# Amid-attention MLP blocks of 384 tokens with the output chunks in two passes over groups of four activation tiles

## The chip, the cores and the metric

The kernel runs on one core of a Trainium2 chip. The metric is the device time in microseconds, the median of three runs. In the core, TensorE (PE) multiplies, VectorE (DVE), ScalarE (ACT) and GpSimd (POOL) work element by element, SyncE (SP) issues most of the DMAs. Each engine runs its instructions in the order in which the program holds them and waits at semaphores for what others produce.

## The reference

Attention with a memory term over 4 batches of 576 tokens and 8 heads of width 64, then two MLPs over the 2304 tokens of 512 values:

```
scores = scale * q @ k.T, causal;  local = softmax(scores) @ v
q_p = phi(q);  mem_out = (q_p @ M_prev) / (q_p . z_prev + 1e-6)
x = g * mem_out + (1 - g) * local                 # (2304, 512)

h = x @ w_in                                      # 512 -> 2048
x = (s * relu(h) ** 2 + b) @ w_out                # 2048 -> 512
h = x @ w2_in
x = (P(h) / (Q(h) + 1e-6)) @ w2_out               # P cubic, Q of |h| and h * h
```

The MLP weights arrive as 64-bit floats and are decoded on the chip. Every MLP operand is split into a high and a low half (type fp32r), and a product is three matmuls: low by high, high by low, high by high.

## The kernel before

Nothing is ordered by hand. The code describes operations (`op`, with the engines that may do them and the planner's cost on each, the tiles read and written, and a due time `plan.at`), and `Plan.run` plays a list schedule: at each step the operation that can start first is placed, ties by due time, and on the engine where it ends first by the planner's costs. So the order on each engine, and for many operations the engine itself, comes out of the planner. The order is fixed when the program is built.

Attention has 32 units (4 batches, a low round of query tiles 0 to 2 and a high round of 3 and 4, 4 head pairs). A unit's names: `s` and `su` scores in PSUM, `p` and `pu` the exponentials, `rs` their sums, `pt` and `th` transposed exponentials in PSUM and SBUF, `qm`, `ph`, `tz`, `c`, `pf`, `fs`, `fl` the phi branch (`fs` and `fl` its high and low half), `mh` and `ml` the halves of the memory matrix, `av` the output in PSUM, `xp` its copy, stored to `xTd`.

While attention runs, the first MLP's first half of hidden features (`wA`: 8 tiles `f` of 128) is worked for the first `NARROW * BA` = 768 tokens, by `block_a`, in blocks of `BA` tokens. A block loads its input (`take`: raw `xr`, halves `xh`, `xl`); `up(f)` makes 12 matmuls into a bank `ha` of PSUM (4 chunks of the input by 3); `relu_square` makes from it `r` on ACT, the square on DVE, the high half `gha` on ACT or DVE, the low half `gla` on DVE; `down` makes 3 matmuls for each of the 4 output chunks into `acc`, summed over the 8 tiles `f`. At the end `acc` is copied to `ev` and stored to `x2p`.

Before, a block has 256 tokens, and two tiles `f` share a bank `ha` side by side, so the element-wise work is 512 wide. The four output chunks share two banks, (0) and (1), two chunks in each, and hold them from the block's first down matmul to its last:

```
                ACC = f"acc{j}_{q}"
                if i == 0:
                    bank(ACC, (q,))
```

All banks but 0 and 1 are free for attention and `ha` (`FREE`). Then `block_wide` does the same for the other 1536 tokens (512 at a time: `hw`, `aw`), `block_b` the second half of the features (`hb`, `ab`), and `block_c` the second MLP (`hc`, `ac`).

Due times: attention's units are `TIMES[0]` apart (1.2 times that in the high rounds); the blocks are due evenly between `FIRST_A` = 90 and the planner's end of attention:

```
    tA = [FIRST_A + k * (END - LAST_A - FIRST_A) / NARROW for k in range(NARROW + 1)]
```

Tiles in SBUF come from rings of named places (`roles`): `gh` 3, `gl` 2, `ev` 2 in the pool `mp`; the pool `at` holds attention's tiles and is closed after it (`swap`).

## Time and profile before

| | us |
|---|---|
| median of 3 runs (1021.85 to 1024.05) | 1023.35 |
| the profiled execution: time | 1023.09 |
| its span, first to last instruction | 1021.3 |
| PE busy in the span | 994.9 |
| DVE, ACT, POOL busy | 840.2, 675.9, 426.3 |
| attention and the amid-attention blocks | about 0 to 290 |
| the other 1536 tokens of the first half | about 290 to 415 |
| the second half of the features | about 415 to 622 |
| the second MLP | about 622 to 1021 |

The page gives busy time by engine. The views of the trace used here: busy time of each engine by stretches (with the number of instructions, the granted TensorE clock as a share of full speed, the share of the DMA engines and their rate), the waits of PE (who waited for whom, total us, times, longest), the chain of work that ended last in order of time, and groups of instructions by line, operation and shape. In these a group's row ends with its busy time, the mean of one in ns, and the idle time of the engine just before. The chain's pieces give the sustained time of a matmul: a run of matmuls by their number. The mean of one matmul is longer, since its pipeline overlaps the next one's.

### The profile page before, as it was taken

What the parts mean: (1) busy time and instruction counts of PE and PEld (TensorE: products, weight loads), DVE (VectorE), ACT (ScalarE), POOL (GpSimd) and SP (SyncE); (2) the same over time, 40 slices, a digit from 0 to 9 for tenths busy, and PEclk for the clock granted to TensorE, in tenths of its full rate; (3) what the DMA queues carried; (4) which work ended last, traced back from release to release, by engine and by line L of the source; (5) the groups of instructions that cost most, each with busy time, mean ns of one, the idle gap of its engine ahead of it and who ended that gap; (6) DMA issues with size and microseconds to landing.
All of it is one profiled execution on the core that took longest, in us unless ns stands there. A gap on an engine that the chain in (4) does not pass through costs nothing.

```text
span 1021.3 us, 16000 instructions
## 1 busy us (share of the span) xinstructions
PE 994.9 (97%) x5356; PEld 828.1 (81%) x5356; DVE 840.2 (82%) x1524; ACT 675.9 (66%) x1419; POOL 426.3 (42%) x494
## 2 busy tenths in 40 slices
PE   7889899999999999999999999999999999999998
PEld 4566687877888888887888998888888888899997
DVE  7999899898858888889887336988888888888895
ACT  6889888677654554444444326777777867877885
POOL 3235344131100100212110006868777876876785
PEclk8999999999999999999999999999999999999999
DMA  7866766554213647767564028401100200100000
GB/s 203 248 210 193 211 202 184 145 157 125 82 49 113 187 145 247 249 201 248 162 210 132 26 84 257 144 1 32 50 1 3 70 1 1 65 2 0 32 1 31
DMA packets 68962, 120.07 MB, mean 118 GB/s; under 512 B 9744, under 2 KB 36880, under 8 KB 68880
## 3 DMA queue, kind: packets, MB, share of 16 engines
q1 hardware_dynamic: 64224, 110.27, 35.2%
q0 software_dynamic: 4224, 8.39, 2.6%
q8 instruction: 42, 0.69, 0.3%
q10 hardware_dynamic: 432, 0.40, 0.1%
q14 instruction: 40, 0.33, 0.1%
HBM read 91.76 MB, written 27.26 MB: 117 GB/s over the span
## 4 chain that ended last, share of the span: by engine, by line
PE 83%; DVE 9%; DMA 3%; ACT 2%; issue 1%; POOL 1%; SPq 0%; DVEq 0%; ACTq 0%; POOLq 0%
PE hc L876 19%; PE ac L1111 19%; PE ab L1025 9%; PE hb L876 8%; PE hw L876 6%; PE aw L988 6%; PE ha L876 3%; PE av L820 3%; PE pt L512 3%; PE acc L949 2%; PE s L640 2%; DVE s L647 1%; PE av L828 1%; DMA qm<-in_vm 1%; PE su L674 1%
## 5 line engine op out<-in xcount | busy, mean ns | idle before, releaser
L1090 DVE RECIPROCAL qe<-qe 128x512 f32<-128x512 f32 (+2 forms) x82 | 242.6, 2958 | 49.2 <-POOL qe L382 49.2
L876 PE MATMUL hc<-xc_h,w2ih 128*128 128x512 f32 (+1 forms) x320 | 117.8, 368 | 0.0
L876 PE MATMUL hc<-xc_h,w2il 128*128 128x512 f32 (+1 forms) x320 | 117.8, 368 | 0.0
L876 PE MATMUL hc<-xc_l,w2ih 128*128 128x512 f32 (+1 forms) x320 | 117.7, 368 | 0.0
L382 POOL TENSOR_TENSOR qe<-qe,qb 128x512 f32<-128x512 f32 (+2 forms) x82 | 94.9, 1157 | 52.4 <-ACT qb L1075 51.3
L1111 PE MATMUL ac<-w2oh,ghc 128*128 128x512 f32 x288 | 112.6, 391 | 0.0
L1111 PE MATMUL ac<-w2ol,ghc 128*128 128x512 f32 x288 | 112.5, 391 | 0.0
L1111 PE MATMUL ac<-w2oh,glc 128*128 128x512 f32 x288 | 112.3, 390 | 0.0
L382 POOL TENSOR_TENSOR glc<-po,ghc 128x512 fp32r<-128x512 f32 (+2 forms) x82 | 95.0, 1158 | 23.3 <-ACT ghc L372 23.1
L382 POOL TENSOR_TENSOR pm<-pm,s 128x512 f32<-128x512 f32 (+2 forms) x82 | 95.5, 1165 | 18.7 <-ACT pm L1075 17.8
L1081 ACT ACTIVATE s<-hc 128x512 f32<-128x512 f32 (+2 forms) x82 | 44.7, 546 | 63.3 <-PE hc L876 60.6
L658 ACT ACTIVATE p<-s,st 128x128 f32<-128x128 f32 (+3 forms) x128 | 67.0, 537 | 19.4 <-DVE st L647 17.5
L1075 ACT ACTIVATE pm<-hc,prm 128x512 f32<-128x512 f32 (+2 forms) x82 | 59.6, 727 | 24.4 <-DVE hc L1092 24.0
L512 PE MATMUL pt<-ident,p 128*128 128x128 f32 x320 | 59.4, 286 | 9.7 <-DVE fl L742 4.7
L876 PEld LDWEIGHTS hc<-xc_h,w2il 128*128 128x128 f32 x320 | 60.1, 188 | 9.0 <-DVE po L1094 0.3
L876 PEld LDWEIGHTS hc<-xc_l,w2ih 128*128 128x128 f32 x320 | 60.1, 188 | 8.5
L876 PEld LDWEIGHTS hc<-xc_h,w2ih 128*128 128x128 f32 x320 | 60.0, 188 | 7.5
L647 DVE CUSTOM_DVE_ANT_0 s<-s,mask 128x128 f32<-128x128 f32 (+3 forms) x128 | 60.4, 507 | 4.6 <-ACT p L658 2.4
L1075 ACT ACTIVATE qb<-s,cq,b1abs 128x512 f32<-128x512 f32 (+2 forms) x82 | 62.7, 764 | 2.1 <-POOL qe L382 2.1
L1111 PEld LDWEIGHTS ac<-w2oh,ghc 128*128 128x128 f32 x288 | 54.1, 188 | 11.4
L1111 PEld LDWEIGHTS ac<-w2oh,glc 128*128 128x128 f32 x288 | 54.1, 188 | 11.1 <-POOL glc L382 0.6
L1111 PEld LDWEIGHTS ac<-w2ol,ghc 128*128 128x128 f32 x288 | 54.1, 188 | 10.4
(488 smaller groups left out, 2795.8 us busy)
## 6 DMA issues: line engine op xcount, KB each, us to landing
qk<-in_qk SPq DMA_DIRECT2D x32, 208.0 KB, 3.9
vm<-in_vm SPq DMA_DIRECT2D x16, 384.0 KB, 4.2
qk<-in_qk SPq DMA_DIRECT2D x30, 192.0 KB, 3.9
out_y<-ob SPq DMA_DIRECT2D x18, 256.0 KB, 2.1
qm<-in_vm SPq DMA_DIRECT2D x16, 256.0 KB, 3.7
w2d<-sh SPq DMA_DIRECT2D x16, 256.0 KB, 4.3
w2d<-sl SPq DMA_DIRECT2D x16, 256.0 KB, 4.0
w2oh<-w2d POOLq DMA_DIRECT2D x4, 1024.0 KB, 16.4
```

The source lines that it names most:

```text
L382: op(ways(c, None, dve, pool), lambda e: e.tensor_tensor(dst(), x(), y(), alu), r, w, port=True)
L512: nc.tensor.transpose(dst[:, o:o + P], src, ident)
L647: e.tensor_tensor_reduce(sp, sp, mask[:, m0:m0 + kb - ka], -scale, 3.0e38 if x == 0 else st[:, t:t + 1], ALU.add, ALU.min, st[:, t + x:t + ...
L658: e.activation(g(f"p{n}_{i}")[:, o:o + kb - ka], g(b)[:, o2:o2 + kb - ka], AF.Exp, scale=-1.0, bias=g(f"st{n}")[:, z_:z_ + 1], accum_out=g ...
L820: nc.tensor.matmul(g(AV)[64 * j:64 * j + 64, ra:rb], g(V)[:, kb, D * j:D * j + D], g(TH)[:, o:o + rb - ra], start=x in firsts, stop=False, ...
L876: nc.tensor.matmul(hs(), m, y, start=c == 0 and k == 0, stop=c == KC - 1 and k == 2)
L988: nc.tensor.matmul(g(ACC)[:, 0:w], outp(y, f)[:, cs], g(z_), start=f == 0 and k == 0, stop=f == HF - 1 and k == 2)
L1025: nc.tensor.matmul(g(ACC)[:, 0:w], outp(y, f)[:, cs], g(z_), start=f == 0 and k == 0, stop=f == HF - 1 and k == 2)
L1075: return lambda e: e.activation(g(dst)[:, ks], g(src)[:, ks], AF.Identity, scale=m, bias=b)
L1081: op(ways(c, -0.04), lambda e, ks=ks: e.activation(g(S2)[:, ks], g(HS)[:, ks], AF.Square), (HS,), part(S2))
L1090: op({"DVE": 0.07 + c * 0.00625}, lambda e, ks=ks: e.reciprocal(g(QE)[:, ks], g(QE)[:, ks]), part(QE), part(QE))
L1111: nc.tensor.matmul(g(ACC), g(x_)[:, ks], g(f"w2o{y}{i}")[:, o], start=f == 0 and q == 0, stop=f == NF - 1 and q == 2)
```

## The change

- A block has 384 tokens, and there are two (`BA`, `NARROW`): the same 768 tokens. A matmul of these blocks has 384 columns for 256.
- Each tile `f` has a bank `ha` of its own, 384 wide; `relu_square` works 384 wide, 16 times for 12.
- An output chunk is 384 wide and fills its own bank. The two banks serve chunks 0 and 1, then 2 and 3, over the tiles `f` 0 to 3 (`GROUP` = 4); then again over 4 to 7. So the halves of four activation tiles stay in SBUF for both passes: `gha` and `gla` have rings of 5, partly in the attention pool.
- After the first group a chunk is copied from PSUM to `ev` (4 tiles of 384); after the second it is added to `ev` by a DVE `tensor_tensor` that reads PSUM and SBUF, and stored.
- `up` and `down` no longer alternate: chunk pairs and ups stand in a list `todo`, due times spread by weight 2 for an up and 1 for a pair of downs.
- Attention's due times are 8.3 apart for 8.5.

```diff
@@ -43,7 +43,7 @@
 LANDS, LANDS_RAW, LANDS_CB = 1.0, 2.5, 2.5
 ALONE = 8
 R0, R1, RN = 0.0, 0.0, 0
-NARROW = 3
+NARROW, GROUP = 2, 4
 LATE = 512, 512, 512
 FIRST_A, LAST_A = 90.0, 0.0
 SOON = 1
@@ -53,7 +53,7 @@
 D0, D1, D2, D3 = 40.0, 5.0, 80.0, 5.0
 TINYPOOL = 0.12
 DIRECT, GATE, MPLAIN = 4, 1.0, 4
-TIMES = 8.5, 8.0, 1.2
+TIMES = 8.3, 8.0, 1.2
 VAL, PHB, BGAP = 1.0, 1.0, 0.15
 DEC = 20.0
 SB0, SB1, SB2, SB3, N2 = 85.0, 25.0, 110.0, 16.0, 8
@@ -270,7 +270,7 @@
     nks = [min(q + P, S) for q in q0s]
     NQ = len(q0s)
     SQ = NQ * P
-    BA = 256
+    BA = 384
 
     pools = {}
 
@@ -313,6 +313,7 @@
         buf(n, None, obj=t)
     both = at.tile([P, 64], F32, name="both")
     nc.vector.tensor_tensor(both, ident[:, 0:64], ident[:, 64:128], ALU.add)
+    at.tile([P, 32], F32, name="fill_at")
     prm = cst.tile([P, 8], F32, name="prm")
     sb = cst.tile([P, 2], F32, name="sb")
     sc1, bi1 = sb[:, 0:1], sb[:, 1:2]
@@ -878,12 +879,12 @@
             first = [] if not c and not part else [(HS, part if c else 0)]
             pe(3 * w, mm, first + [XH, XL, kh, kl], ((HS, part),), 3)
 
-    def relu_square(HS, hs, w, nm):
+    def relu_square(HS, hs, w, nm, gh="gh", gl="gl"):
 
         R, GH, GL = f"r{nm}", f"gh{nm}", f"gl{nm}"
         ring(R, "r", [P, w], F32)
-        ring(GH, "gh", [P, w], F32R)
-        ring(GL, "gl", [P, w], F32R)
+        ring(GH, gh, [P, w], F32R)
+        ring(GL, gl, [P, w], F32R)
 
         def relu(e):
             e.activation(g(R), hs(), AF.Relu)
@@ -915,51 +916,60 @@
 
     def block_a(j, at0, at1, inp, outp):
 
-        t0 = j * BA
+        t0, w = j * BA, BA
         plan.at = at0 - LOADS
-        x = take(f"xa{j}", BA, tok_runs(t0, BA))
+        x = take(f"xa{j}", w, tok_runs(t0, w))
         parts = {}
 
-        def up(i):
-            HS = f"ha{j}_{i}"
+        def up(f):
+            HS = f"ha{j}_{f}"
             bank(HS, FREE)
-            for u in range(2):
-                f = 2 * i + u
-                fs = slice(f * P, (f + 1) * P)
-                up_matmuls(HS, lambda u=u: g(HS)[:, u * BA:(u + 1) * BA], BA, x,
-                           lambda c, f=f: (("w1ihA", (c, f // 4)), ("w1ilA", (c, f // 4))),
-                           lambda y, c, fs=fs: inp(y, c, fs), u)
-            parts[i] = relu_square(HS, lambda: g(HS), 512, f"a{j}_{i}")
-
-        def down(i):
-            GH, GL = parts[i]
-            for q in range(2):
-                ACC = f"acc{j}_{q}"
-                if i == 0:
-                    bank(ACC, (q,))
-                for c in (2 * q, 2 * q + 1):
-                    cs = slice(c * P, (c + 1) * P)
-                    for u in range(2):
-                        f = 2 * i + u
-
-                        def mm(ACC=ACC, c=c, cs=cs, u=u, f=f):
-                            a = g(ACC)[:, (c % 2) * BA:(c % 2 + 1) * BA]
-                            us = slice(u * BA, (u + 1) * BA)
-                            for k, (y, z_) in enumerate((("l", GH), ("h", GL), ("h", GH))):
-                                nc.tensor.matmul(a, outp(y, f)[:, cs], g(z_)[:, us],
-                                                 start=f == 0 and k == 0 and c % 2 == 0,
-                                                 stop=f == HF - 1 and k == 2, skip_group_check=True)
-
-                        first = f == 0 and c % 2 == 0
-                        pe(3 * BA, mm, ([] if first else [ACC]) + [GH, GL, ("w1ohA", f), ("w1olA", f)], (ACC,), 3)
-                if i == HF // 2 - 1:
-                    EV = f"ev{j}_{q}"
-                    ring(EV, "ev", [P, 512], F32)
-                    copy(lambda EV=EV: g(EV), lambda ACC=ACC: g(ACC), 512, (ACC,), (EV,), act=-0.04)
-                    load(lambda q=q: x2p[q * 2 * P:(q + 1) * 2 * P, t0:t0 + BA].rearrange("(c p) t -> p c t", p=P),
-                         lambda EV=EV: g(EV).rearrange("p (c t) -> p c t", c=2), 512 * 512, (EV,), (("x2p", j),))
-
-        interleave(HF // 2, 1, up, down, at0, at1)
+            fs = slice(f * P, (f + 1) * P)
+            up_matmuls(HS, lambda: g(HS)[:, 0:w], w, x, lambda c: (("w1ihA", (c, f // 4)), ("w1ilA", (c, f // 4))),
+                       lambda y, c: inp(y, c, fs))
+            parts[f] = relu_square(HS, lambda: g(HS)[:, 0:w], w, f"a{j}_{f}", "gha", "gla")
+
+        def down(f, cs):
+            GH, GL = parts[f]
+            h, k4 = divmod(f, GROUP)
+            for c in cs:
+                ACC, EV = f"acc{j}_{h}_{c}", f"ev{j}_{c}"
+                ms = slice(c * P, (c + 1) * P)
+                if k4 == 0:
+                    bank(ACC, (c % 2,))
+
+                def mm(ACC=ACC, ms=ms):
+                    for k, (y, z_) in enumerate((("l", GH), ("h", GL), ("h", GH))):
+                        nc.tensor.matmul(g(ACC)[:, 0:w], outp(y, f)[:, ms], g(z_), start=k4 == 0 and k == 0,
+                                         stop=k4 == GROUP - 1 and k == 2)
+
+                pe(3 * w, mm, ([ACC] if k4 else []) + [GH, GL, ("w1ohA", f), ("w1olA", f)], (ACC,), 3)
+                if k4 < GROUP - 1:
+                    continue
+                if h == 0:
+                    ring(EV, "eva", [P, w], F32)
+                    copy(lambda EV=EV: g(EV), lambda ACC=ACC: g(ACC)[:, 0:w], w, (ACC,), (EV,), act=-0.04)
+                else:
+                    op(ways(w, None, 1.0), lambda e, ACC=ACC, EV=EV: e.tensor_tensor(
+                        g(EV), g(ACC)[:, 0:w], g(EV), ALU.add), (ACC, EV), (EV,))
+                if h == HF // GROUP - 1:
+                    load(lambda c=c: x2p[c * P:(c + 1) * P, t0:t0 + w], lambda EV=EV: g(EV), 512 * w, (EV,), (("x2p", j),))
+
+        todo = [(up, (0,))]
+        for h in range(HF // GROUP):
+            f0 = h * GROUP
+            for f in range(f0, f0 + GROUP):
+                if h == 0 and f + 1 < GROUP:
+                    todo.append((up, (f + 1,)))
+                todo.append((down, (f, (0, 1))))
+            for f in range(f0, f0 + GROUP):
+                if f + GROUP < HF:
+                    todo.append((up, (f + GROUP,)))
+                todo.append((down, (f, (2, 3))))
+        cost = [2.0 if fn is up else 1.0 for fn, _ in todo]
+        for i, (fn, args) in enumerate(todo):
+            plan.at = at0 + (at1 - at0) * sum(cost[:i]) / sum(cost)
+            fn(*args)
 
     def block_wide(t0, w, at0, at1, inp, outp):
 
@@ -1128,6 +1138,9 @@
         "gh": [("mp", f"gh{i}") for i in range(3)], "gl": [("mp", f"gl{i}") for i in range(2)],
         "r": [("mp", "r")], "ev": [("mp", f"ev{i}") for i in range(2)],
     })
+    roles["gha"] = [("mp", "gh0"), ("mp", "gh1"), ("mp", "gh2")] + [("at", f"gx{i}") for i in range(GROUP - 2)]
+    roles["gla"] = [("mp", "gl0"), ("mp", "gl1")] + [("at", f"gy{i}") for i in range(GROUP - 1)]
+    roles["eva"] = [("mp", "ev0"), ("mp", "ev1"), ("at", "ex0"), ("at", "ex1")]
     NPR = len(units)
 
     TL, TS, TR = TIMES
```

In the built program PE has 192 matmuls fewer: 576 of 256 columns in the blocks become 384 of 384. Of this stage's element-wise instructions, DVE has 863 before and 848 now, ACT 565 and 578, POOL 177 and 209; the loads of block input are 8 and 12, the stores 6 and 8.

Two places in the order. First PE at the end of the last block. Before, its last down matmuls (`acc`, chunks 2 and 3 in bank 1) stand among the last unit's steps:

```order
L949 MATMUL acc_1_3852<-gha_3_4292,w1olA 128x256
L949 MATMUL acc_1_3852<-gla_3_4303,w1ohA 128x256
L949 MATMUL acc_1_3852<-gha_3_4292,w1ohA 128x256
L949 MATMUL acc_1_3852<-gha_3_4292,w1olA 128x256
L949 MATMUL acc_1_3852<-gla_3_4303,w1ohA 128x256
L949 MATMUL acc_1_3852<-gha_3_4292,w1ohA 128x256
L512 MATMUL pt_0_4448<-ident,p_0_4367 128x128
L791 MATMUL pt_0_4448<-ident,pu_4401 128x2x64
L512 MATMUL pt_0_4448<-ident,p_0_4380 128x128
L512 MATMUL pt_0_4448<-ident,pu_4401 128x128
```

Now, at the same end, `acc_1_0` and `acc_1_1` (second group, chunks 0 and 1) get their last matmuls, and a few rows later `acc_1_2` opens on the bank that `acc_1_0` held (lines are those of the changed kernel):

```order
L943 MATMUL acc_1_0_4128<-gha_7_4052,w1ohA 128x384
L943 MATMUL acc_1_1_4139<-gha_7_4052,w1olA 128x384
L943 MATMUL acc_1_1_4139<-gla_7_4069,w1ohA 128x384
L943 MATMUL acc_1_1_4139<-gha_7_4052,w1ohA 128x384
L513 MATMUL pf_4266<-ident,ph_4082 128x128
L736 MATMUL pf_4266<-both,ph_4082 128x64
L877 MATMUL hw_0_4269<-xw_h_4006,w1ilA 128x512
L877 MATMUL hw_0_4269<-xw_l_4021,w1ihA 128x512
L877 MATMUL hw_0_4269<-xw_h_4006,w1ihA 128x512
L943 MATMUL acc_1_2_4282<-gha_4_3566,w1olA 128x384
```

What moved: a bank that was held through the block now changes its tenant here, with three block matmuls, two phi transposes and three wide matmuls between.

Second, DVE at the same place, from the last unit's transposed exponentials (`th`) to the first wide block (`hw`). Before:

```order
L374 COPY th_2_4385<-pt_2_4370 128x384
L677 ISA su_1_4363,su_4374<-su_1_4363,mask_87,su_4374 128x288
L677 ISA su_4374 128x1
L742 TENSOR_TENSOR fl_4403<-pf_4382,fs_4396 128x192
L691 TENSOR_TENSOR rs_4368<-rs_4368 128x2
L694 TENSOR_SCALAR rs_4368<-rs_4368 128x2x2
L695 RECIPROCAL rs_4368<-rs_4368 128x2x2
L696 TENSOR_TENSOR rs_4368<-rs_4368,omg_112 128x2x2
L706 TENSOR_SCALAR p_0_4367<-p_0_4367,rs_4368 128x512
L706 TENSOR_SCALAR pu_4401<-pu_4401,rs_4368 128x576
L892 SCALAR_TENSOR_TENSOR hw_0_4472<-hw_0_4472,sb,rw_0_4510 128x512
```

Now:

```order
L375 COPY th_2_4252<-pt_2_4241 128x384
L375 COPY th_3_4259<-pt_3_4248 128x384
L953 TENSOR_TENSOR ev_0_3496<-acc_1_0_4128,ev_0_3496 128x384
L953 TENSOR_TENSOR ev_1_3501<-acc_1_1_4139,ev_1_3501 128x384
L743 TENSOR_TENSOR fl_4280<-pf_4266,fs_4276 128x192
L696 RECIPROCAL rs_4237<-rs_4237 128x2x2
L697 TENSOR_TENSOR rs_4237<-rs_4237,omg_113 128x2x2
L707 TENSOR_SCALAR p_0_4236<-p_0_4236,rs_4237 128x512
L707 TENSOR_SCALAR pu_4257<-pu_4257,rs_4237 128x576
L953 TENSOR_TENSOR ev_2_4004<-acc_1_2_4282,ev_2_4004 128x384
L953 TENSOR_TENSOR ev_3_4076<-acc_1_3_4305,ev_3_4076 128x384
L893 SCALAR_TENSOR_TENSOR hw_0_4269<-hw_0_4269,sb,rw_0_4389 128x512
```

What moved: four adds stand in DVE's row, two of them ahead of phi's low half and the last unit's scalings; two small steps on the sums went to POOL.

## Rows read from the trace of the kernel before

**Rows 1.** Page, part 1: busy us, share of the span, instructions.
```profile
PE 994.9 (97%) x5356; PEld 828.1 (81%) x5356; DVE 840.2 (82%) x1524; ACT 675.9 (66%) x1419; POOL 426.3 (42%) x494
```

**Rows 2.** Busy time by stretches of the first 290 us, columns in its head.
```profile
core 0: us, PE busy (x) PEld busy (x) DVE busy (x) ACT busy (x) POOL busy (x), PEclk, DMA share, GB/s
0.00:16.00 16.00, 9.15 (x38) 5.28 (x38) 9.37 (x51) 7.84 (x26) 5.85 (x21) 0.95 0.87 256
16.00:125.00 109.00, 98.86 (x673) 70.90 (x672) 103.20 (x338) 96.23 (x278) 39.38 (x90) 0.96 0.72 206
125.00:160.00 35.00, 32.10 (x270) 26.86 (x272) 33.85 (x107) 30.98 (x86) 17.28 (x28) 1.00 0.68 204
160.00:290.00 130.00, 127.97 (x996) 103.60 (x993) 110.40 (x383) 92.09 (x261) 24.49 (x53) 1.00 0.45 128
```

**Rows 3.** What PE waited for, 16 to 160 us: total, times, longest.
```profile
PE pt L512 <- DVE fl L742: 3.6, 4, 1.4
PE pt L512 <- ACT p L658: 3.5, 4, 2.5
```

**Rows 4.** The same, 160 to 290 us.
```profile
PE pt L512 <- DVE fl L742: 1.1, 2, 0.6
PE ha L876 <- ACT th L372: 0.6, 1, 0.6
PE av L820 <- PE pt L512: 0.3, 1, 0.3
```

**Rows 5.** Pieces of the chain: start us, us, what.
```profile
155.99 2.15 PE acc L949 x18
...
196.03 2.88 PE ha L876 x24
...
299.35 2.72 PE aw L988 x12
...
952.82 2.10 PE hc L876 x12
...
965.35 4.18 PE hc L876 x24
```

**Rows 6.** DVE instructions of 0 to 290 us by shape: busy us, mean ns, idle before.
```profile
L374 DVE COPY th<-pt 128x384 f32<-128x384 f32 x25 | 13.5, 545 | 0.0
...
L892 DVE SCALAR_TENSOR_TENSOR ha<-ha,sb,ra 128x512 f32<-128x512 f32 x12 | 9.0, 749 | 0.5 <-ACT ra L889 0.5
...
L742 DVE TENSOR_TENSOR fl<-pf,fs 128x384 fp32r<-128x384 f32 x12 | 6.6, 550 | 0.4 <-ACT fs L372 0.4
...
L382 DVE TENSOR_TENSOR tz<-ph,zb 128x256 f32<-128x256 f32 x14 | 6.1, 436 | 0.2
...
L706 DVE TENSOR_SCALAR p<-p,rs 128x256 f32<-128x256 f32 x17 | 5.3, 348 | 0.0
...
L706 DVE TENSOR_SCALAR p<-p,rs 128x384 f32<-128x384 f32 x12 | 5.2, 438 | 0.0
...
L706 DVE TENSOR_SCALAR p<-p,rs 128x128 f32<-128x128 f32 x15 | 3.9, 282 | 0.1
...
L382 DVE TENSOR_TENSOR ml<-vm,mh 128x128 fp32r<-128x128 f32 x13 | 3.7, 288 | 0.2
...
L590 DVE TENSOR_SCALAR qm<-qm 128x384 f32<-128x384 f32 x6 | 2.1, 355 | 1.9 <-ACT ph L584 1.8
...
L898 DVE TENSOR_SCALAR gha<-ha,sb 128x512 fp32r<-128x512 f32 x2 | 1.5, 747 | 0.0
```

**Rows 7.** POOL of the same stretch, and DVE's weight decode, by shape.
```profile
L382 POOL TENSOR_TENSOR tz<-ph,zb 128x256 f32<-128x256 f32 x2 | 1.5, 726 | 7.0 <-DVE ph L595 6.9
...
L382 POOL TENSOR_TENSOR ml<-vm,mh 128x128 fp32r<-128x128 f32 x3 | 1.7, 579 | 3.5 <-ACT mh L372 3.5
...
L434 DVE SCALAR_TENSOR_TENSOR dAo4f<-dAo4r,dAo4f 128x512 int32<-128x512 int32 x1 | 0.8, 770 | 0.0
...
L434 DVE SCALAR_TENSOR_TENSOR dAi_1f<-dAi_1r,dAi_1f 128x512 int32<-128x512 int32 x4 | 2.7, 682 | 0.0
```

## The prediction

> **What bounds the kernel now.** The page first [rows 1]: PE is busy 97% of the span, DVE 82%. A busy PE need not be PE at its peak, so the stages are read apart. From about 295 us the chain of waits is nearly all PE, twelve 512-column matmuls in 2.72 us [rows 5], and nothing there is edited: the last 2161 matmuls stand in the same order in both kernels, and between them and the attention stage the same matmuls stand, a few of them some places earlier or later. So the question is how long the first 290 us take.
>
> The table by stretches [rows 2] cuts them in three. From 0 to 16 us data arrives. From 16 to 160 us DVE is busy 103.2 of 109 and 33.9 of 35 us, and PE is idle 109 - 98.9 = 10.1 and 35 - 32.1 = 2.9 us, 13.0 together: DVE is late there, and PE waits for what DVE and ACT bring, which the waits say too [rows 3]: transposes wait for the low half of phi (DVE, 0.9 us each) and for the exponentials (ACT). From 160 to 290 us PE is busy 128.0 of 130 us while DVE has 20 us to spare, and all of PE's waits come to 2.0 us [rows 4]. So a microsecond of PE work that is removed is worth a microsecond after 160 us, and before it only if the idle PE doesn't swallow it. A microsecond of DVE work counts before 160 us only.
>
> **PE: fewer matmuls for the same columns.** Both kernels send 147,456 columns through the amid-attention blocks: 576 matmuls of 256 columns, now 384 of 384. In unbroken runs a 256-column matmul takes 2.15/18 = 0.1194 us and 2.88/24 = 0.1200 us, and a 384-column one 2.10/12 = 0.1750 and 4.18/24 = 0.1742 us [rows 5]. So 576 x 0.1197 = 68.9 us becomes 384 x 0.1745 = 67.0 us: **1.9 us off PE**. Each matmul costs about 13 ns over its columns' time at 2.4 GHz (256 columns: 106.7 ns), and 192 matmuls fewer save that. The interleaving with attention's 64-row matmuls changes little: 59 separate runs of block matmuls before, 63 now. I count these 1.9 us in full, because the same columns end in a stage where PE is the bound.
>
> The Trainium skill (TensorE: Matmul & The Clock Gate, "Wait — 56ns, not 53.3ns?") gives a warm matmul a fixed cost of about 2.5 ns over its columns. By that, 192 matmuls fewer would save 0.5 us; the trace shows about 13 ns each [rows 5], so the measurement decides, and what is left of the page's figure is a rival below.
>
> **DVE: what is added and what the planner moves away.** Added on DVE, by forms of the same width in the trace [rows 6]: 8 adds of an output chunk in PSUM to its tile in SBUF, 384 wide, at the 550 ns of the phi low half, which also reads PSUM and SBUF: 4.4 us. 3 of the 8 first-pass copies (ACT did all 6 before) at 545 ns: 1.6 us. The high half of the activation on DVE 5 times at 384 columns for 2 times at 512: 5 x 0.56 - 2 x 0.75 = 1.3 us. The two activation passes cost the same: 24 x 0.75 = 18.0 us before, 32 x 0.56 = 17.9 now, since 384 columns take three quarters of 512. So 7.3 us more. But the planner deals with it: by the order, 7 transposed-score copies leave DVE (7 x 0.545 = 3.8), 12 scalings of the exponentials (4 x 0.282 + 5 x 0.348 + 3 x 0.438 = 4.2), 9 low halves of the memory matrix (about 9 x 0.30 = 2.7), 5 products of phi with z (5 x 0.436 = 2.2) and 4 of the plus-one passes (4 x 0.355 = 1.4): 14.3 us. The other moves are one to four short instructions each, both ways, and are taken to cancel. Net, DVE has **7.0 us less** of 257 before 290 us.
>
> POOL takes most of it, 209 instructions of this stage for 177, and is slower at each: the phi product takes it 726 ns for 436, the memory low half 579 for 288 [rows 7]. It has the time (87 us busy of 290), but what goes through it comes later to the next reader.
>
> How much of the 7.0 us reaches the end? Spread evenly, 144/274 of it, 3.7 us, falls in the stretch from 16 to 160 us where DVE is late. The upper end is then 3.7 us gained; the lower is nothing, or a loss if POOL's longer steps stand in the chain. A second reading comes from the order of the matmuls: ahead of the 64th of attention's 128 score matmuls stand 114 of the 576 block matmuls before (13.6 us) and 96 of the 384 now (16.8 us). So 3.1 us more block work is offered to PE while it idles; at the 72nd the lead is 24.6 to 23.7 us, 0.9 us. Between 0.9 and 3.1, and with POOL's delay against it, I take **1.5 us**, with 0 and 3.7 as ends.
>
> **PSUM: the two banks of the output chunks change hands more often.** Before, two banks hold all four chunks of a block from its first to its last down matmul: 6 tenants, and 4 times a new one follows within these blocks. Now each chunk holds a bank for one group of four activation tiles: 16 tenants, 14 changes. At each the next first matmul waits until the copy or the add has read the bank. By the order, PE has other work between an old tenant's last matmul and a new one's first; the shortest such covers are 2.7 us at the end of the first block, and 2.4 and 1.4 us at the end of the second (the shown place: 3 block matmuls at 0.174, two phi transposes of about 0.1, 3 wide ones at 0.227 [rows 5]), the others 3.2 to 13 us. An add needs its 0.55 us after a matmul's tail of about 0.3 us, so 1.4 us covers it if DVE is free, and DVE is free after 160 us. Where it isn't, the price of one such wait is what PE pays now for a PSUM reader on DVE, 0.55 us on average late [rows 4] and 0.9 us early [rows 3]. Bounds: 0, and 3 x 0.9 = 2.7 us. I take **0.4 us lost**, near the free end, since two of the three stand at the end of the stage, where PE is the bound.
>
> Other edits cost nothing here: 12 loads of block input for 8 and 8 stores for 6 lie under a DMA that is no bound after 160 us (45% busy [rows 2]); the planner's cadence 8.3 for 8.5 only shifts places in the order, already counted in it; new tiles in the attention pool take space alone. The first 115 matmuls are the same.
>
> **Sum**, against the profiled execution's own 1023.09 us (median of the runs 1023.35, so the two are 0.03% apart): -1.9 - 1.5 + 0.4 = -3.0, so **1020.1 us**.
>
> **Rivals.**
> 1. *Adds in DVE's queue hold up attention* (slower). DVE runs in order, and an add that waits for its chunk's last matmul holds what is queued behind: at the shown place phi's low half, the last unit's reciprocal and its scalings, on which PE's next transposes wait. The first block's adds stand where DVE is still nearly full. Price: 8 adds, each with the 0.9 us that PE now waits for DVE [rows 3], is 7.2 us; with the gains of 3.4 us that is +3.8, **1026.9 us**. It decides from 3.4/8 = 0.43 us per add on. For it: DVE's early load. Against: after 160 us DVE is idle 20 of 130 us.
> 2. *POOL's new share slows DVE* (no change). In the trace a DVE pass of the weight decode takes 770 ns once and 682 ns otherwise [rows 7]. If each of the 32 added POOL instructions costs DVE those 0.09 us, that is 2.9 us, and the 1.5 us gained turn into 1.4 lost: -1.9 + 1.4 + 0.4 = -0.1, **1023.0 us**. The Trainium skill (SBUF — State Buffer, "Who interferes with whom") says that a DVE instruction with two SBUF inputs and a GpSimd one that reads SBUF exclude each other, whichever comes second waiting for all of the first; that is the direction of this rival, and no row here shows a whole block of that length.
> 3. *Only the matmuls gain* (no change). The lead in block work is given back at the end: after the last score matmul 30 block matmuls are left now, 5.2 us, for 24, 2.9 us, before. Then -1.9 + 0.4 = -1.5, **1021.6 us**.
> 4. *DVE's relief counts in full* (faster still): -1.9 - 7.0 + 0.4 = -8.5, **1014.6 us**. For it: the early stage has 13.0 us of PE idle. Against: half of the relief falls after 160 us.
> 5. *The fixed cost per matmul is small*: 0.5 us instead of 1.9 in the sum gives -1.6, **1021.5 us**; that is what the page's figure cited above would make of it, and the runs at both widths [rows 5] speak against it.
>
> That the change doesn't do what it says is out: the order shows 384 matmuls for 576 and the adds in place.
>
> **How the numbers follow.** The forecast (1017 to 1021.3 us) has 0.42, rival 4 0.13: faster by over 0.2% (2.05 us, about what can be told from no change) 0.55. Rival 3 has 0.12, rival 2 0.10, rival 5 0.03: 0.25 within 0.2%. Rival 1 has 0.20, slower. The range of 8 in 10 must reach the DVE bound below (1014.5, just at rival 4) and rival 1's price above (1027).
>
> **What would show it.** Right: block matmuls at 0.174 us each, PE's waits from 160 us to the first wide block still near 2 us, that block's steady run beginning about 3 us earlier than before, later stages shifted unchanged. The early stage: PE idle from 16 to 160 us down from 13.0 to about 11.5 us. Wrong: rows of PE waiting on the adds or on first-pass copies (rival 1), DVE passes longer by 0.1 us with POOL beside them (rival 2), or more PE idle before 160 us than now. If a long PE gap in the early stage took the granted clock down again, as in 16 to 125 us now (0.96 [rows 2]), some us would be lost that no term holds.

## The result: 1013.1 us, faster than forecast

The changed kernel takes 1013.12 us (median of 6 runs, 1012.04 to 1017.16), the kernel before beside it 1023.09 (6 runs, 1021.85 to 1024.22): a ratio of 0.991, 95% interval 0.9894 to 0.9925. That is 10.0 us gained where 3.0 were forecast; the direction was right, the time lies 1.4 us below the range. The profiled execution took 1013.53 us with a span of 1011.7, against 1023.09 and 1021.3 before, so 9.6 us is what the traces can explain.

Part 1 of the page after, to be held against [rows 1]:

```profile
PE 991.6 (98%) x5164; PEld 821.8 (81%) x5164; DVE 840.4 (83%) x1513; ACT 678.4 (67%) x1431; POOL 439.5 (43%) x523
```

PE is busy 3.3 us less, DVE the same over the whole span, POOL 13 us more. The stretches of the first 290 us after, with the columns of [rows 2]:

```profile
core 0: us, PE busy (x) PEld busy (x) DVE busy (x) ACT busy (x) POOL busy (x), PEclk, DMA share, GB/s
0.00:16.00 16.00, 9.31 (x38) 5.55 (x38) 9.26 (x51) 7.84 (x26) 5.74 (x21) 0.93 0.83 241
16.00:125.00 109.00, 102.32 (x668) 72.28 (x669) 106.22 (x351) 100.50 (x289) 45.08 (x98) 0.96 0.73 210
125.00:160.00 35.00, 33.48 (x248) 26.40 (x245) 34.45 (x112) 32.97 (x100) 17.60 (x30) 1.00 0.64 194
160.00:290.00 130.00, 128.66 (x885) 102.91 (x884) 106.68 (x356) 90.33 (x252) 34.21 (x73) 1.00 0.46 132
```

From 16 to 160 us PE is idle 6.7 + 1.5 = 8.2 us for 13.0 before, and from 160 to 290 us 1.3 for 2.0. DVE is not freer in the early stretch but fuller: 106.2 of 109 us for 103.2 [rows 2], 34.5 of 35 for 33.9. So DVE's own idle time there fell from 6.9 to 3.3 us. This is the first sign against the forecast's picture of a DVE that was full of work: before, part of its early time was waiting.

PE's waits after, in the stretches 16 to 125, 125 to 160 and 160 to 290 us (who waited, for whom: total us, times, longest):

```profile
PE su L675 <- ACT fs L373: 2.5, 1, 2.5
PE pf L513 <- ACT p L659: 1.6, 1, 1.6
PE pt L513 <- DVE fl L743: 0.9, 1, 0.9
...
PE pt L513 <- DVE fl L743: 0.6, 1, 0.6
PE pt L513 <- ACT p L659: 0.5, 1, 0.5
...
PE pt L513 <- DVE fl L743: 1.0, 2, 0.7
PE s L641 <- ACT p L659: 0.2, 1, 0.2
```

Against [rows 3, 4]: the transposes' waits for the low half of phi are 0.9 + 0.6 us early for 3.6, those for the exponentials shorter too. The longest wait, 2.5 us of `su` for phi's high half on ACT, is new; before, the longest was 2.5 us for the exponentials. No row has PE waiting for an output chunk's copy or add.

Where the stages now stand, by the matmuls of each (columns: count, duration ns min/median/max, first and last start in us), first before, then after:

```profile
L876 PE MATMUL hw<-xw_h,w1ilA x96: 389/389/474, 290.1 to 416.9; 128*128 128x512 f32 x96
L876 PE MATMUL hb<-xb_h,w1ilB x160: 333/389/389, 420.3 to 617.1; 128*128 128x512 f32 x96, 128*128 128x384 f32 x64
```
```profile
L877 PE MATMUL hw<-xw_h,w1ilA x96: 389/389/476, 273.9 to 408.8; 128*128 128x512 f32 x96
L877 PE MATMUL hb<-xb_h,w1ilB x160: 333/389/389, 412.2 to 607.9; 128*128 128x512 f32 x96, 128*128 128x384 f32 x64
```

The wide block ends 8.1 us earlier (the first `hw` matmul starts 16 us earlier, since now some are placed ahead of attention's end; the last one tells the shift), and the second half of the features begins 8.1 and ends 9.2 us earlier. Of the 9.6 us of the traces all but 1.5 are thus made by the end of the wide block: 1.1 more come in the second half of the features, 0.4 behind it.

### The profile page after: what moved, and what is told of

Read it like the earlier page. It is cut to its first block, busy times and chain, and to the rows that moved or that the text cites. A ratio compares the mean times of both kernels' runs of the same rounds, so it can differ in the third digit from the quotient of the medians.

```text
span 1011.7 us, 15688 instructions
## 1 busy us (share of the span) xinstructions
PE 991.6 (98%) x5164; PEld 821.8 (81%) x5164; DVE 840.4 (83%) x1513; ACT 678.4 (67%) x1431; POOL 439.5 (43%) x523
## 4 chain that ended last, share of the span: by engine, by line
PE 85%; DVE 6%; ACT 4%; DMA 2%; issue 1%; POOL 1%; SPq 0%; DVEq 0%; ACTq 0%; POOLq 0%
PE hc L877 20%; PE ac L1121 20%; PE ab L1035 9%; PE hb L877 9%; PE hw L877 6%; PE aw L998 6%; PE av L821 3%; PE pt L513 3%; PE acc L943 2%; PE ha L877 2%; PE s L641 2%; ACT p L659 1%; PE av L829 1%; DVE s L648 1%; PE su L675 1%
## 5 line engine op out<-in xcount | busy, mean ns | idle before, releaser
L1121 PEld LDWEIGHTS ac<-w2ol,ghc 128*128 128x128 f32 x288 | 54.0, 188 | 10.5
```

The lines of the kernel that those rows point to most:

```text
L1121: nc.tensor.matmul(g(ACC), g(x_)[:, ks], g(f"w2o{y}{i}")[:, o], start=f == 0 and q == 0, stop=f == NF - 1 and q == 2)
```

## The experiments

Three questions were to be told apart: is it that DVE has less to do (its load); that block work is offered to PE earlier (its lead); or that a single wait was lost? Medians of the kernel before, run beside these, lie between 1022.65 and 1023.57 us. DVE's work ahead of a place in the program is summed from a trace as the time from each DVE instruction's start to the next one's, less DVE's idle time; the place used is the 80th of attention's 128 masked score passes. Ahead of it DVE has 147.6 us of work and 12.6 of idle before, 143.3 and 8.9 after; the pass itself starts at 160.8 us before and at 152.8 after. So on DVE these 8.0 us are 4.3 us of work and 3.7 us of waiting.

**The cadence alone, in either kernel.**

```diff
-TIMES = 8.3, 8.0, 1.2
+TIMES = 8.5, 8.0, 1.2      # a_cadence85: in the kernel after
```

> The changed kernel with attention's due times 8.5 apart again, all else as changed. By the order it loses DVE's relief (DVE work of the stage 319.2 us by the rows of before, for 318.3 before and 310.6 changed) but keeps, and widens, the lead in block matmuls (19.3 us of them ahead of the 64th score matmul, for 13.6 before and 16.7 changed). Theory 1, DVE's relief made the gain beyond the 1.9 us of fewer matmuls: about 1020 us. Theory 2, block matmuls offered earlier fill PE's idle time: about 1013 us, as the changed kernel. Theory 3, the cadence alone made it: as before, 1021 to 1023 us.

Measured 1021.13 us (ratio 0.997, 0.996 to 0.9981). With attention at 8.5 apart the block's change gains only 2.4 us.

```diff
-TIMES = 8.5, 8.0, 1.2
+TIMES = 8.3, 8.0, 1.2      # b_cadence83: in the kernel before
```

> The kernel before with the cadence 8.3 alone: three blocks of 256 tokens, one pass. By the order DVE has 323 us of work in the stage for 318, and the lead at the 64th score matmul is the same 13.6 us. Theory 1 (DVE's load): slower than before, 1025 us. Theory 2 (lead): as before, 1023 us. Theory 3 (the cadence alone): about 1015 us.

Measured 1031.82 us (1.0087, 1.0068 to 1.0107): the cadence that gains 8.0 us in the kernel after costs 8.7 us in the one before. So neither part is the gain by itself; what matters is the order into which the two fall. The lead in block work at the 64th score matmul does not go with the times: it is 19.3 us with 8.5 in the kernel after, more than the 16.7 of after, and 13.6 with 8.3 in the kernel before, the same as with 8.5. The lead alone is not the cause. DVE's work ahead of the 80th masked pass is 4.0 us more than before in the first run and 7.6 us more in the second. That fits the second run's loss, but the first has more of it than before and is still 2.4 us faster.

**The old block width in the new structure.**

```diff
-NARROW, GROUP = 2, 4
+NARROW, GROUP = 3, 4
-    BA = 384
+    BA = 256
```

> The changed kernel with three blocks of 256 tokens: two passes over groups of four tiles and the adds as changed, matmuls of 256 columns again (576 of them), element-wise work 256 wide. By the order the lead at the 64th score matmul is 18.6 us, DVE's work 319 us. Theory 1: 1.9 us for the matmuls and some 5 for DVE's load more than the changed kernel, about 1020 us. Theory 2: 1.9 us more than the changed kernel, about 1015 us.

Measured 1026.55 us (1.0038, 1.0024 to 1.0052). With 256 columns, in the order that the planner makes of them, the passes over groups bring nothing; DVE has 158.9 us of work ahead of the 80th masked pass, 11 more than before.

**Three changed orders of the kernel after.**

```diff
-FIRST_A, LAST_A = 90.0, 0.0
+FIRST_A, LAST_A = 80.0, 0.0     # a_first80; 100.0 in a_first100
```
```diff
-TIMES = 8.3, 8.0, 1.2
+TIMES = 8.25, 8.0, 1.2          # a_cadence825
```

> The changed kernel with the first block due at 80 for 90. By the order it has the same DVE work as the changed kernel (310.3 us for 310.6 by the rows of before) and a little more lead (18.3 us of block matmuls ahead of the 64th score matmul for 16.7), but other steps on other places. Theory 1: 1012 to 1014 us. Theory 2 (the lead): 1012 us. Theory 4 (the gain is this one order's luck): back to 1018 to 1022 us.

> The changed kernel with the cadence 8.25: another order, DVE's work 311.6 us for 310.6, up to the 72nd mask 171.5 us for 173.9, lead 16.7 us as changed. Theory 1: 1012 to 1015 us. Theory 4 (this one order's luck): 1017 to 1022 us.

> The kernel after with the blocks due from 100 for 90. DVE's stage work is 311.6 us for 310.6, ahead of the 80th masked score pass 185.7 for 180.2, and the lead in block work at the 64th and 72nd score matmul 15.1 and 22.4 us for 16.7 and 24.5. Theory A by the early work alone: 5.5 x 0.85, about 1018 us (but the cadence 8.25 had 185.1 there and gave 1013.5, so this form of it has that run against it). By the work of the whole stage: 1013.5 to 1014 us. Theory C, the lead counted in full: 1.6 to 2.1 us more, 1015 us.

Measured 1013.63, 1013.5 and 1014.78 us. The gain is not the luck of one order: three neighbouring settings keep it, though the fourth, the cadence 8.5 above, does not. They also speak against a simple count of DVE's load: ahead of the 80th masked pass DVE has 146.6, 147.5 and 145.5 us of work in them, 0.1 to 2.1 us less than before, and yet 8 to 9 us are gained. In a_first80 PE's idle time from 16 to 160 us is 8.4 + 1.0 = 9.4 us:

```profile
16.00:125.00 109.00, 100.58 (x660) 71.99 (x661) 107.27 (x348) 98.27 (x280) 49.01 (x100) 0.97 0.73 208
125.00:160.00 35.00, 34.03 (x246) 26.95 (x245) 33.99 (x112) 31.61 (x95) 14.81 (x29) 1.00 0.67 195
```

**The adds made thin.**

```diff
-    g(EV), g(ACC)[:, 0:w], g(EV), ALU.add), (ACC, EV), (EV,))
+    g(EV)[:, 0:8], g(ACC)[:, 0:8], g(EV)[:, 0:8], ALU.add), (ACC, EV), (EV,))
```

> The changed kernel in its own order with the 8 adds cut to 8 columns (of 384; the second group's sums then reach the output in those columns alone), about 0.35 us each, 2.8 us less DVE work, the waits of the banks as they are. Theory 1: 0.5 to 2 us faster than the changed kernel, 1011 to 1012.5 us. Theory 2, and if the adds stand where nothing waits: within 0.7 us of the changed kernel.

Measured 1013.59 us: the length of the eight adds costs nothing that can be measured. What an add waits for was left as it is.

**DVE's load at a fixed order: taken away in before, added in after.**

```diff
+                    if e is nc.vector and b - a <= 384:
+                        x = g(name)[:, a:a + 8]
                     e.tensor_scalar(x, x, g(RS)[:, c[0], c[1]:c[1] + 1], 0.0, ALU.mult, ALU.add)
```

> The kernel before in the same order, with the 44 scalings of exponentials of 128 to 384 columns that stand on DVE cut to 8 columns (the rest of those tiles stays unscaled): some 8 us less DVE work, nothing else moved, planner untouched. Theory 1 (DVE's relief counts in full where PE waits, before 160 us): 4 to 6 us faster, 1017 to 1019 us. Theory 2 (DVE's load isn't what held PE): within 1.5 us of before, 1022 to 1023 us.

Measured 1023.09 us (1.0001, 0.9985 to 1.0017): no gain. The relief was smaller than the 8 us expected: from start to start the 44 scalings take 6.1 us for 11.8, so 5.8 us less, and only 2.9 of these lie ahead of the 80th masked pass. The windows of its profile show why the run can't price even that. PE's idle time from 16 to 160 us is 8.7 + 2.2 = 10.9 us, 2.1 less than before, but the granted clock is lower, 0.92 for 0.96 and 0.97 for 1.00:

```profile
16.00:125.00 109.00, 100.34 (x669) 72.79 (x669) 100.38 (x340) 96.15 (x277) 40.55 (x90) 0.92 0.71 206
125.00:160.00 35.00, 32.82 (x271) 27.80 (x270) 33.89 (x106) 30.89 (x85) 16.77 (x26) 0.97 0.68 204
```

And the dummies in the kernel after (`fill` is the 128x32 tile of the change; its first value and the count of the scalings are left out here):

```diff
                     e.tensor_scalar(x, x, g(RS)[:, c[0], c[1]:c[1] + 1], 0.0, ALU.mult, ALU.add)
+                    if e is nc.vector:
+                        e.tensor_scalar(fill, fill, 1.0, 0.0, ALU.mult, ALU.add)
# a_dve_early: two dummies each, behind the first 22 of these scalings only
# a_dve_late: two dummies each, behind all but the first 30
```

> The changed kernel in its own order, with one small DVE instruction more (32 columns on a tile of its own) behind each of the 52 scalings of exponentials that stand on DVE: 52 x about 0.17 us, some 9 us of DVE work put back, nothing moved. Theory 1 (DVE's relief is most of the gain): 3 to 8 us slower than the changed kernel, 1016 to 1021 us. Theory 2 (the gain lies in which steps stand ahead of which, not in DVE's load): 1013 to 1015 us.

> The kernel after in its own order, with 44 dummy DVE passes of 32 columns (0.173 us each in the run with dummies, 7.6 us together) put behind the first 22 DVE scalings of the exponentials; all but one stand ahead of the 80th of the 128 masked score passes. Counted with durations of the kernel before, DVE's work ahead of that pass is 189.5 us before and 180.2 us after, so nearly the whole relief lies early. Theory A (DVE is the bound early, and what is taken off it there counts nearly whole): about 0.85 of 7.6, 1013.1 + 6.5 = 1019.6 us. Theory B (DVE's work counts 0.42 wherever it lies in the stage, as the evenly spread dummies gave): 1013.1 + 3.2 = 1016.3 us. Theory C (the gain is the order of PE's work, with DVE's load of little weight): 1014 us.

> The same 7.6 us of dummy DVE passes, all but one behind the 96th masked score pass, where DVE is no longer full. Theory A: next to nothing, 1013 to 1014 us. Theory B: 1016.3 us as for the early ones. Theory C: 1013 to 1014 us.

Measured 1016.82 us with 52 spread dummies, 1020.22 with 44 early ones, 1018.12 with 44 late ones. The spread ones occupy DVE for 7.2 us (start to start) and cost 3.7, 0.5 per microsecond. The early ones occupy it for 7.8 us and cost 1020.22 - 1013.12 = 7.1 us, 0.9 per microsecond; the late ones occupy it for 6.6 us and cost 5.0. So adding to DVE early is paid nearly whole, and the theory's other half falls: the late ones, put in pairs into the last third of attention, weren't free either. There DVE has little to spare: in the kernel after it is busy 53.9 of the 60 us from 205 to 265 us. In the run with early dummies DVE is no busier than after (106.4 and 34.3 us); what it was given stands in PE's idle time, 10.2 + 2.5 = 12.7 us for 8.2:

```profile
16.00:125.00 109.00, 98.80 (x636) 69.53 (x636) 106.35 (x369) 96.94 (x277) 43.11 (x93) 0.96 0.68 194
125.00:160.00 35.00, 32.54 (x238) 26.44 (x236) 34.32 (x111) 30.48 (x89) 16.40 (x29) 1.00 0.67 207
```

**Two products kept off POOL.** The product of phi and z and the low half of the memory matrix are 31 instructions on POOL in the kernel after and 17 in the kernel before; here they are none, and the planner makes a new order.

```diff
-    ... ALU.mult, c, (F, Z), (T,))
+    ... ALU.mult, c, (F, Z), (T,), pool=None)
-    ... ALU.subtract, P, (MB, MH), (ML,))
+    ... ALU.subtract, P, (MB, MH), (ML,), pool=None)
```

> The kernel after with the product of phi and z and the low half of the memory matrix kept off POOL (13 and 18 instructions there); the planner orders anew. DVE's stage work by durations of before is 325.4 us for 310.6, its work ahead of the 80th masked score pass 193.0 for 180.2; the block work offered by the 64th and 72nd score matmul is the same (16.7 and 24.0 us for 16.7 and 24.5). Theory A (early DVE work): 12.8 x 0.85 = 10.9, about 1024 us. Theory B: 14.8 x 0.42 = 6.2, about 1019 us. Theory C (lead in block work): unchanged, 1013 to 1014 us; and 1 to 2 us less than that if POOL's slow steps stand in the chain.

Measured 1017.08 us (0.9942, 0.9924 to 0.996). POOL's share with the order around it is worth 4.0 us, between the theories. DVE has 148.7 us of work ahead of the 80th masked pass, 5.4 more than after, so 0.7 per microsecond. That is 1.1 us more than in the kernel before, and the run is still 5.6 us faster than before: a good half of the gain comes without less early work for DVE. The 12.8 us of the expectation counted whole durations, of which some 80 ns in each DVE instruction overlap the next. PE is idle 8.4 + 3.0 = 11.4 us from 16 to 160 us:

```profile
16.00:125.00 109.00, 100.57 (x658) 72.12 (x659) 106.09 (x367) 101.02 (x293) 37.48 (x80) 0.97 0.72 211
125.00:160.00 35.00, 31.98 (x232) 25.02 (x230) 34.31 (x116) 30.20 (x84) 13.22 (x21) 1.00 0.65 186
```

**One wait in the kernel before.** The forecast did not ask what DVE, ACT and PE waited for from 110 to 125 us in the kernel before (DVE's waits, then ACT's, then PE's, then the window, then the issue of the load, then how long the two loads of `prm` took to land):

```profile
DVE w1ilA L382 <- ACT w1ihA L372: 3.0, 1, 3.0
...
ACT b1abs L1191 <- DMA prm<-in_b: 2.7, 1, 2.7
...
PE ha L876 <- DVE w1ilA L382: 1.0, 1, 1.0
PE pt L512 <- ACT p L658: 0.6, 1, 0.6
...
110.00:125.00 15.00, 12.76 (x96) 9.43 (x94) 11.98 (x36) 11.20 (x31) 4.75 (x9) 1.00 0.75 221
...
L1187 SPq DMA_DIRECT2D prm<-in_b x1: 422/422/422, 113.3 to 113.3; - x1
...
DMA to landing us min/median/max: 5.1/5.2/5.3
```

The chain of the same kernel, the view of [rows 5], has the load as well, with the two steps behind it:

```profile
113.34 5.10 DMA prm<-in_b
118.57 0.61 ACT w1ihA L372
119.21 0.69 DVE w1ilA L382
```

`prm` holds six parameters of the second MLP, `b1abs` the absolute value of one of them, not used before 620 us. The load is issued at 113.3 us, ACT reaches `b1abs` at 115.8 us and waits 2.7 us for it to land. Behind it in ACT's queue stands a weight's high half (`w1ihA`), for that DVE waits 3.0 us with all its queue behind, and PE is idle 15 - 12.8 = 2.2 us. In the kernel after the same load is issued at 111.6 us, lands in 2.6 us, half the time, and `b1abs` comes at 114.8 us without a wait; from 110 to 125 us PE is busy throughout:

```profile
L1200 SPq DMA_DIRECT2D prm<-in_b x1: 430/430/430, 111.6 to 111.6; - x1
L1204 ACT ACTIVATE b1abs<-prm x1: 235/235/235, 114.8 to 114.8; 128x1 f32<-128x1 f32 x1
...
DMA to landing us min/median/max: 2.6/2.6/2.6
...
110.00:125.00 15.00, 15.00 (x105) 11.80 (x103) 14.53 (x50) 13.29 (x37) 6.80 (x13) 1.00 0.81 218
```

So the two small loads were issued in the kernel before some 90 us earlier, with every other instruction where it was:

```diff
     def scale_bias(e):
         for t, x in ((s1, sc1), (b1, bi1)):
             e.dma_start(x, t.rearrange("(o h) -> o h", o=1).to_broadcast([P, 1]))
+        for t, o, n in ((a2, 2, 4), (b2, 6, 2)):
+            e.dma_start(prm[:, o:o + n], t.rearrange("(o h) -> o h", o=1).to_broadcast([P, n]))
...
     def params(e):
-        for t, o, n in ((a2, 2, 4), (b2, 6, 2)):
-            e.dma_start(prm[:, o:o + n], t.rearrange("(o h) -> o h", o=1).to_broadcast([P, n]))
+        pass
```

> The kernel before with the two small loads of prm (4 and 2 parameters) issued on SP about 90 us earlier, behind those of the scale and bias; every other instruction on every engine stands where it stood. ACT's wait of 2.7 us at b1abs goes, and with it the 3.0 us that DVE waits for ACT's w1ihA. Theory D (this wait is about 3 us of the gain): 1022.9 - 2.5 to 3.0 = about 1020.1 us. Theory E (the time that ACT and DVE gain is lost again at the next wait of PE, or TensorE's clock takes it back): 1022 to 1023 us.

> The same with the 44 narrowed DVE scalings of the earlier run (a part of the softmax scaling is left out). Theory D with DVE's relief: 1023 - 2.8 (the wait) - 3.7 (the relief at equal granted clock) = 1016.5 us, which with the matmuls' 1.9 us would be the whole gain of the change. If the relief only turns into idle time of DVE, as it did in that run: 1020 us.

Measured 1020.47 us (0.998, 0.9969 to 0.999) and, with the narrowed scalings as well, 1019.43 (0.9967, 0.9954 to 0.998). The one wait is 2.5 us of the kernel before, with 1.0 to 3.2 as the interval. PE's idle time from 16 to 160 us is 8.4 + 2.1 = 10.5 us, 2.5 less, and from 110 to 125 us 0.8 for 2.2:

```profile
16.00:125.00 109.00, 100.58 (x677) 72.46 (x677) 105.11 (x345) 98.19 (x284) 40.35 (x90) 0.95 0.72 209
125.00:160.00 35.00, 32.88 (x279) 27.40 (x278) 33.80 (x110) 30.66 (x85) 17.95 (x29) 1.00 0.67 204
...
110.00:125.00 15.00, 14.18 (x107) 10.83 (x106) 14.77 (x45) 13.99 (x39) 5.53 (x10) 1.00 0.81 239
```

The relief of DVE, 2.9 us ahead of the 80th masked pass, brings only another 1.0 us on top, not 3.7; the expectation's 1016.5 is missed by 2.9 us. In the earlier run with narrowed scalings the wait at `b1abs` was still there, 3.2 us long.

The wait put back into the kernel after, as work of ACT:

```diff
+    def b1_abs(e):
+        for _ in range(16):
+            e.activation(fill, fill, AF.Abs)
+        e.activation(b1abs, prm[:, 7:8], AF.Abs)
-    op(ways(1, 0.0), lambda e: e.activation(b1abs, prm[:, 7:8], AF.Abs), ("prm",), ("prm",))
+    op(ways(1, 0.0), b1_abs, ("prm",), ("prm",))
```

> The kernel after with 16 dummy ACT passes of 32 columns ahead of the b1abs pass (about 0.1 to 0.2 us each, 1.6 to 3.2 us together), at about 115 us, where the kernel before has its wait. Theory D: the time grows by nearly the stall, to 1015 to 1016 us. Theory E: 1013 to 1014 us.

Measured 1019.18 us (0.9964, 0.9952 to 0.9975). The sixteen passes took more than meant, 114.2 to 118.4 us, so 4.2 us of stall cost 6.1. The stall is longer than the wait it stands for, so it can't price that wait. It begins as in the kernel before, with DVE waiting for ACT's `w1ihA`; PE's longest wait is here for ACT itself, and then the clock adds to it (the dummies; DVE's longest wait; PE's; two windows):

```profile
L1207 ACT ACTIVATE fill_at<-fill_at x16: 229/229/242, 114.2 to 118.2; 128x32 f32<-128x32 f32 x16
...
DVE w1ilA L384 <- ACT w1ihA L374: 3.8, 1, 3.8
...
PE pt L793 <- ACT pu L706: 2.7, 1, 2.7
...
110.00:118.00 8.00, 6.52 (x49) 4.90 (x48) 6.04 (x21) 7.32 (x27) 2.59 (x5) 1.00 0.68 151
...
118.40:125.00 6.60, 5.78 (x19) 5.00 (x20) 4.07 (x11) 5.53 (x16) 2.75 (x3) 0.50 0.61 213
```

## Why the prediction was wrong, by its own steps

**What bounds the kernel.** Right as to the place: but for 1.5 us the gain is made by the end of the wide block, and the largest part of it is PE's idle time before 160 us. Wrong as to what stood behind that idle time. The step "DVE is late there" was read from DVE's busy share and from PE's waits alone. DVE's 6.9 us of idle time in that stretch stood in [rows 2] beside the 103.2 and 33.9 us, and who caused it was not asked. The largest piece was DVE waiting 3.0 us for ACT, which waited for a load, and the chain of the kernel before held both. Wrong also is that DVE's work counts before 160 us only: the late dummies cost 5.0 us. PE's idle time there fell by 4.8 us, and 2.5 of these are what the moved load alone gives in the kernel before.

**Fewer matmuls, -1.9.** Borne out in size by the chain after, where 18 matmuls of 384 columns follow each other in 3.15 us and 12 in 2.10 (columns: start in us, length, engine, tile, line, number):

```profile
174.08 3.15 PE acc L943 x18
...
187.93 2.10 PE ha L877 x12
...
263.63 2.62 PE acc L943 x15
```

That is 0.175 us each, as the forecast had it from [rows 5]. No run isolates it; the 2.4 us that are left when the cadence is 8.5 are near it, but that run lacks the wait at `b1abs` as well. Rival 5 falls with it. By the figure of the Trainium skill (TensorE: Matmul & The Clock Gate, "Wait — 56ns, not 53.3ns?"), about 2.5 ns over the columns' time, a matmul here would take 0.1625 us, an estimate from that figure; the chain does not agree.

**DVE's relief and the lead, -1.5 with ends 0 and 3.7.** This is the step that failed. Two errors are in it. The price: 7.0 us of relief were "spread evenly" and counted only for the half before 160 us, then cut to 1.5 for POOL's delay. The 7.0 was itself a little large: the 32 activation passes of 384 columns were put at 0.56 us and take 616 and 606 ns, 1.6 us more in all. The dummies price DVE's work at 0.9 per microsecond early, 0.8 late (5.0 / 6.6) and 0.5 spread, and POOL's share turns out to be worth 4.0 us instead of costing something. And the sort: the gain was sought in instructions that leave DVE. By DVE's own time the 80th masked pass starts 8.0 us earlier, 4.3 us by less work, near the upper end of 3.7, and 3.7 us by less waiting, which no term holds. A new order from the planner also decides which waits fall where, and one such wait, worth 2.5 us, stood in the order of before by accident. The term had no room for it, since a planner's order is not a sum of moved instructions.

**The banks of the output chunks, +0.4.** Zero. The change's 14 hand-overs of a bank leave no row among PE's waits, and thin adds change nothing.

**Later stages shifted unchanged.** Nearly. In the second half of the features another 1.1 us is gained. The windows from 425 to 470 us, before and after, differ by 0.4 us of PE's idle time, and one wait of PE of before is not there after; the other 0.7 us are not explained:

```profile
425.00:470.00 45.00, 44.46 (x195) 36.06 (x194) 39.05 (x60) 19.03 (x32) 10.27 (x10) 1.00 0.67 212
...
PE ab L1025 <- DVE glb L901: 0.5, 2, 0.3
```
```profile
425.00:470.00 45.00, 44.87 (x199) 36.78 (x198) 38.35 (x61) 19.59 (x32) 6.23 (x6) 1.00 0.66 212
```

**The rivals.** Rival 1 (adds hold up attention): no wait of PE in the trace, and thin adds give 1013.59 us. An add does hold DVE once, for 5.8 us up to 282 us, but behind it stand only the block's last add and the wide block:

```profile
DVE ev L953 <- PE acc L943: 5.8, 1, 5.8
```

Rival 2 (POOL slows DVE): the sign is the other way, 4.0 us lost without POOL's share. The mean of the 32 masked passes over 512 columns is 705 ns after and 704 ns without that share, by the groups of DVE's instructions. The Trainium skill's rule on the shared port (SBUF — State Buffer, "Who interferes with whom") concerns passes with two inputs from SBUF: for the phi pass of 384 columns (`ph` from `ph` and `qm`) the groups have 606 ns after and 553 ns without POOL's share, which is its direction and small beside the gain. For the product of phi and z, which has two such inputs as well, they have 554 and 550 ns, so this pass does not show it. Rival 3 (lead given back): no. Rival 4 (relief in full) came within 1.5 us of the time, but by another way: DVE's work ahead of the 80th masked pass is 4.3 us less, not 7.0, and orders with nearly none of that relief are as fast. That its number came so near is luck.

**What adds up and what stays open.** On PE: 1.9 us fewer matmul time, 4.8 us less idle time from 16 to 160 us, 0.7 from 160 to 290, 0.4 at the transition, together 7.8 of 9.6 us. Of the 4.8, 2.5 are put down to the lost wait: taking it away in the kernel before gives that much. That it adds up with the rest in the kernel after is argued, not shown. The other 2.3 are put down to the new order; DVE's load has a part in them, as the dummies and POOL's share show, but the orders of a_first80 and a_cadence825 reach the same time with hardly less early DVE work, and taking DVE work out of before gave 0 and 1.0 us. How they divide is not settled. Nor are the 1.8 us that are left: 1.4 by which PE's busy time fell beyond the blocks' own matmuls (3.3 less 1.9), and 0.4 of idle time elsewhere. The wait at `b1abs` is also absent with the cadence 8.5 in the kernel after (1021.13 us), with 256 columns in the new structure (1026.55) and with the cadence 8.3 in the kernel before (1031.82); so it is a part of the account and no key to it. One rival stays untested: of the kernel before only one other setting was run, 8.7 us slower, so how much of the 10 us is the planner's scatter from one order to the next is not known.

## What to carry to other kernels

Where a planner makes the order, cost its result by the waits as well as by the instructions that move: read the idle time of the engine that seems to be full, name what ended each piece of a microsecond or more, and ask which of them the new order keeps. A tiny load whose value is needed much later can hold an in-order queue, and the engine behind it, in the middle of the busiest stage; issue such loads early. And try a change with two or three neighbouring settings of its tuning number, since the same cadence gained 8.0 us in one kernel and cost 8.7 in the other.

## What the runs showed of the hardware

In these traces idle time of PE can cost twice. In the run with narrowed scalings PE was busy 1.24 of the 3.70 us before 51.7 us, and the granted clock of the next stretch was 0.51, which is the lower level, 1.2 GHz:

```profile
48.00:51.70 3.70, 1.24 (x9) 1.01 (x10) 3.70 (x12) 2.15 (x7) 0.23 (x1) 1.00 0.97 309
51.70:55.00 3.30, 3.30 (x11) 2.30 (x10) 3.30 (x9) 2.97 (x9) 0.43 (x2) 0.51 0.43 144
```

The kernel before shows the same at 69 us, where PE had been busy 1.05 of 3 us. In the run with ACT's dummies the stretch behind the stall is at 0.50 for 6.6 us, in the kernel before, with 2.2 us of idle time at the same place, it stayed at 1.00. So the 4.2 us stall cost 6.1 us. By the pages its span is 4.6 us longer than after, and 2.5 of these are longer busy time of PE over the same matmuls (994.1 us for 991.6).

A relief that shifts PE's gaps can lose at the clock what it gains in idle time. With narrowed scalings the same 5356 matmuls keep PE busy 2.7 us longer than before [rows 1], and PE is idle 2.8 us less in a span of 1021.2 us for 1021.3. Its wait at `b1abs` and the stretch behind that are a part of it (the page's first line, ACT's wait, the window):

```profile
PE 997.6 (98%) x5356; PEld 831.2 (81%) x5356; DVE 834.9 (82%) x1524; ACT 676.5 (66%) x1419; POOL 427.1 (42%) x494
...
ACT b1abs L1193 <- DMA prm<-in_b: 3.2, 1, 3.2
...
123.50:127.00 3.50, 3.50 (x17) 2.94 (x15) 3.50 (x10) 3.03 (x9) 1.04 (x3) 0.52 0.51 151
```

The times vary with the clock too: of the ten runs with narrowed scalings, by their mean granted clock, those at 0.989 to 0.990 took 1023.0 to 1025.5 us, those at 0.991 to 0.993 took 1021.3 to 1023.2, and of the two at 0.995 one took 1019.2 and the other, against the series, 1027.1.
